# A fused attention, LayerNorm, MLP and expert kernel: k and q are loaded where their places come free, q's parts get a second home, chained products keep to four banks, and the ring of streamed weights has five places

## The chip, the cores and the metric

The kernel runs on one core of a Trainium2 chip. The metric is the device time of one execution in microseconds (us), taken as the median of several runs. A core has a matrix engine (TensorE, PE in the rows), a vector engine (VectorE, DVE), a scalar engine (ScalarE, ACT), GpSimd (POOL) and SyncE (SP), which here only issues transfers (DMAs). Each engine has an instruction queue of its own and waits for the others by semaphores.

## The reference

Three layers follow each other on 8 batches of 576 rows; all numbers are float32.

```python
def _attn_ref(q, k, v):                  # 8 batches, 8 heads, 576 x 64
    q_s = softmax(q, axis=-1)            # over the 64 of a head
    k_s = softmax(k, axis=2)             # over the 576 rows
    kv = np.einsum('bhsd,bhse->bhde', k_s, v)
    return np.einsum('bhsd,bhde->bhse', q_s, kv)

def _moe_ref(x, g_ln, w_ch1, w_ch2):     # x: 8 x 576 x 512
    mu = np.mean(x, axis=-1, keepdims=True)
    var = np.mean((x - mu) ** 2, axis=-1, keepdims=True)
    xn = (x - mu) / np.sqrt(var + 1e-06) * g_ln
    ch = np.maximum(xn @ w_ch1, 0.0) @ w_ch2      # 512 to 2048 to 512
    return x + ch
...
# third layer: 4 causal attention heads as experts, of which each row takes its best 2
```

## The kernel before, in words

Every float32 operand of a product is split into two rounded halves, so that a product is three matmuls (high by high, high by low, low by high). The matmul that fills most of the time has 128x128 weights and 128x288 moving columns, 288 being half (h = 0, 1) of a batch's rows.

**Units.** A head pair of a batch is a unit, n = 4 x batch + pair (class Heads). Its work comes in six steps: row maxima of k, softmax of k (k_exp writes ke), softmax of q (q_scale writes qe for head j = 0 and 1), turning q (pq, then qT = its high part by ACT and its low part by DVE), kv_product (pkv, at whose start the last 128 rows of q are turned too), then po, the pair's result. v has two homes, one for even and one for odd units. kv_product ends by issuing the loads of k, q and v of the unit two further on; these go through SyncE, whose queue keeps the written order (manual_schedule). The other engines' instructions are put in order by the framework's scheduler.

**LayerNorm** (class Norm) works on one half at a time: pmu (the mean by a matmul), the squares (ACT, added on GpSimd), pvar, root, scaling, and then class Mix, which makes the sums of blocks that the MLP needs (b11, t1, t2, b22, t3, b21, t4; tiles xm, xw_a, xw_b). front_slots says at which slots of the previous batch's matmul pieces the steps of units and LayerNorm are called: NORM_GAP = 8 slots lie between the two halves.

**MLP.** The hidden layer has 16 blocks of 128. From batch 2 (FAST) on, 12 of them are done by Strassen-Winograd with 7 products in place of 8, in three groups of four blocks (fast_group). A product j (0 to 6) for i = 0, 1 is six matmuls. Products chain in three accumulators: pa (j = 0, 2, 4, 6), pc (j = 1, 3), pb (j = 5). DVE adds parts that ACT copied before (total, tmp), ACT takes relu and the rounded high part, DVE or GpSimd the low part: these are the hidden parts hid0 and hid1. Behind each group, `second` sums eight accumulators of 12 matmuls each from four hidden parts, and DVE adds each one to xT. bank() hands PSUM banks to pa, pb, pc and acc in rotation over six.

**Streamed weights.** The weights of a group's seven products are sums of weight blocks, made once (class Sums, its pieces pinned into the slots of batch 1) and kept in device memory as w_d. They are read again for each batch, 21 per batch, through a ring of six places (class Stream); fill(), called behind each product, issues loads as long as their places are free. I write W0, W1, ... for them: W28 to W34 are the seven of batch 3's group 1.

In time: batch 0 and 1 take the first 237 us, batches 2 to 7 follow until about 775 us, and the third layer takes the rest, which the diff doesn't touch.

## Time and profile before

| what | value |
|---|---|
| median of 3 runs | 1348.7 us (1347.04 to 1350.21) |
| profiled execution, its own time | 1347.08 us |
| its span, first to last instruction | 1345.4 us |
| mean granted TensorE clock | 0.992 |
| PE busy | 1289.7 us (96%) |
| DVE, ACT, POOL busy | 956.9 (71%), 762.0 (57%), 460.6 us (34%) |

The span is what the trace covers; the execution's own time is 1.7 us longer. PE is busy for 96% of it, so a change of the order can win only what PE waits, and what it loses when its clock is lowered.

### The profile page before, as it was taken

Reading aid. Unit: us, or ns where it says so; the run is one execution under the profiler, and the core shown is the slowest. Engines: PE = TensorE matmul, PEld = TensorE weight load, DVE = VectorE, ACT = ScalarE, POOL = GpSimd, SP = SyncE. Lnnn points to the kernel's source line nnn. Section 1 sums busy time; section 2 is a strip of 40 time slices with the busy share of each in tenths; the row PEclk is TensorE's granted clock in tenths of the full one; section 3 lists DMA queues with packets and bytes.
Section 4 is the critical chain, followed back from the end, with each engine's and each line's share of the span. In section 5 each row is a group of like instructions: output and inputs, shape, how many; then the busy total and the mean of one; then the engine's idle time right before and its main releaser. Section 6 shows DMA issues by size and latency. Waiting matters only on the chain.

```text
span 1345.4 us, 27550 instructions
## 1 busy us (share of the span) xinstructions
PE 1289.7 (96%) x9907; PEld 1239.7 (92%) x9907; DVE 956.9 (71%) x2704; ACT 762.0 (57%) x1956; POOL 460.6 (34%) x568
## 2 busy tenths in 40 slices
PE   6999999699989999999998999999999999999998
PEld 5889999699979999999998999999999999999996
DVE  6885776866858769678487447777777777777774
ACT  6875444544555556455466235656565666666665
POOL 6675345433444335434346101112121112121222
PEclk9999999899989999999999999999999999999999
DMA  9763375965755657657458224333323242333122
GB/s 244 222 213 96 120 250 168 321 184 176 236 174 193 211 184 256 193 200 237 126 194 279 64 62 139 87 110 86 106 73 104 81 110 94 90 107 91 44 50 73
DMA packets 173416, 203.53 MB, mean 151 GB/s; under 512 B 93152, under 2 KB 137696, under 8 KB 170976
## 3 DMA queue, kind: packets, MB, share of 16 engines
q1 hardware_dynamic: 150656, 164.80, 41.0%
q10 hardware_dynamic: 22624, 36.97, 7.5%
q8 instruction: 79, 1.29, 0.4%
q14 instruction: 57, 0.47, 0.1%
HBM read 140.13 MB, written 46.40 MB: 139 GB/s over the span
## 4 chain that ended last, share of the span: by engine, by line
PE 67%; DVE 11%; DMA 7%; ACT 3%; issue 2%; POOL 2%; SPq 1%; ACTq 0%; DVEq 0%; POOLq 0%
PE acc L191 14%; PE psh L191 11%; PE psqk L191 7%; PE psc L191 7%; PE pssc L191 4%; PE pa L194 4%; PE py L191 4%; PE pso L191 4%; PE psv L191 4%; PE pst L1827 3%; DMA q<-in_q_dram 2%; PE pc L194 2%; DVE xc L692 1%; DMA k<-in_k_dram 1%; DMA wraw<-in_moe_w_ch_dram 1%
## 5 line engine op out<-in xcount | busy, mean ns | idle before, releaser
L191 PE MATMUL psh<-xhl,w 128*128 128x288 f32 x1248 | 188.6, 298 | 1.3 <-DVE xhl L701 1.0
L191 PEld LDWEIGHTS psh<-xhl,w 128*128 128x128 f32 x1248 | 172.2, 188 | 3.9 <-DVE xhl L701 1.5
L1810 POOL TENSOR_SCALAR sm<-sm,st,lg 128x128 f32<-128x128 f32 (+3 forms) x128 | 82.5, 655 | 263.7 <-DVE lg L1727 62.3
L191 PE MATMUL acc<-xw_b,w 128*128 128x288 f32 x912 | 137.4, 298 | 5.6 <-POOL xw_b L1325 3.4
L191 PE MATMUL acc<-xw_a,w 128*128 128x288 f32 x912 | 138.5, 297 | 3.4 <-DVE tmp L1328 1.7
L191 PEld LDWEIGHTS acc<-xw_b,w 128*128 128x128 f32 x912 | 125.7, 188 | 8.2 <-POOL xw_b L1325 4.8
L191 PEld LDWEIGHTS acc<-xw_a,w 128*128 128x128 f32 x912 | 126.3, 188 | 5.0 <-DVE xw_a L313 2.9
L191 PE MATMUL psqk<-x,wqk 128*128 128x288 f32 x768 | 112.9, 297 | 0.4 <-DVE k L1630 0.4
L191 PEld LDWEIGHTS psqk<-x,wqk 128*128 128x128 f32 x768 | 105.1, 188 | 1.6 <-PE pst L1827 0.6
L1391 DVE TENSOR_TENSOR xT<-xT,acc 128x288 f32<-128x288 f32 x152 | 66.2, 448 | 50.0 <-PE acc L191 49.6
L191 PE MATMUL psc<-hb,w 128*128 128x288 f32 x672 | 100.2, 298 | 0.0
L1798 ACT ACTIVATE sm<-sm,st 128x128 f32<-128x128 f32 (+3 forms) x144 | 83.9, 584 | 20.5 <-DVE st L1790 19.0
L191 PEld LDWEIGHTS psc<-hb,w 128*128 128x128 f32 x672 | 92.1, 188 | 0.3
L191 PE MATMUL acc<-hh,w 128*128 128x288 f32 x576 | 89.3, 300 | 2.9 <-DVE hh L798 1.5
L191 PEld LDWEIGHTS acc<-hh,w 128*128 128x128 f32 x576 | 79.8, 188 | 6.2 <-DVE hh L798 3.0
L1325 POOL TENSOR_TENSOR xw_b<-tmp,xw_b 128x288 fp32r<-128x288 f32 x72 | 61.3, 864 | 69.2 <-ACT xw_b L1324 49.9
L1851 ACT ACTIVATE aTh<-pst 128x128 fp32r<-128x128 f32 (+4 forms) x224 | 70.2, 333 | 23.4 <-PE pst L1827 10.9
L1852 DVE TENSOR_TENSOR aTl<-pst,aTh 128x384 fp32r<-128x384 f32 (+3 forms) x196 | 72.4, 381 | 11.4 <-ACT aTh L1851 9.0
L1790 DVE CUSTOM_DVE_ANT_0 sm<-pssc,mask 128x128 f32<-128x128 f32 (+2 forms) x144 | 67.9, 482 | 15.7 <-PE pssc L191 6.5
L645 POOL TENSOR_TENSOR sq<-sq 128x288 f32<-128x288 f32 x42 | 37.5, 894 | 91.0 <-ACT sq L676 89.0
L507 POOL TENSOR_TENSOR qe<-q,sm 128x320 f32<-128x320 f32 x64 | 46.8, 751 | 43.9 <-PE pkv L546 30.5
L191 PE MATMUL pssc<-k,q 128*128 128x128 f32 (+3 forms) x256 | 59.2, 327 | 0.0
(268 smaller groups left out, 3160.7 us busy)
## 6 DMA issues: line engine op xcount, KB each, us to landing
w_r<-w_d SPq DMA_DIRECT2D x76, 512.0 KB, 5.2
xw_b<-w_d SPq DMA_DIRECT2D x42, 512.0 KB, 4.8
wraw<-in_moe_w_ch_dram SPq DMA_DIRECT2D x32, 512.0 KB, 4.6
xhl<-xn_d SPq DMA_DIRECT2D x14, 1152.0 KB, 5.0
xp_d<-xT ACTq DMA_DIRECT2D x16, 576.0 KB, 5.0
k<-k SPq DMA_DIRECT2D x32, 288.0 KB, 3.5
k<-in_k_dram SPq DMA_DIRECT2D x32, 256.0 KB, 3.6
q<-in_q_dram SPq DMA_DIRECT2D x32, 256.0 KB, 4.0
```

The lines of the kernel that those rows point to most:

```text
L191: nc.tensor.matmul(o, lhsT, rhs, start=start, stop=stop)
L194: nc.tensor.matmul(o, lhsT, rhs, start=start, stop=stop, skip_group_check=True)
L507: nc.gpsimd.tensor_tensor(self.qe[:, :, j, :], self.qt[:, j], self.sm[:, 2, j * NCH:(j + 1) * NCH, None].to_broadcast([P, NCH, D]), op=ALU ...
L645: nc.gpsimd.tensor_tensor(self.t, self.t, self.sq[:, c], op=ALU.add)
L1325: nc.gpsimd.tensor_tensor(u[:, 1], src, raw(u[:, 0]), op=ALU.subtract)
L1391: nc.vector.tensor_tensor(xs[:, c], xs[:, c], ps, op=ALU.add)
L1790: nc.vector.tensor_tensor_reduce(out=sm[:m, c0:c1], in0=o_, in1=msk, scale=1.0, scalar=3e38 if n == 0 else st[:m, j, 0:1], op0=ALU.add, op ...
L1798: nc.scalar.activation(sm[:m, :w], sm[:m, :w], AF.Exp, bias=st[:m, j, last:last + 1], scale=-1.0, accum_out=st[:m, j, 2:3])
L1810: nc.gpsimd.tensor_scalar(sm[:m, :w], sm[:m, :w], st[:m, j, 3:4], self.gate()[:, j:j + 1], op0=ALU.mult, op1=ALU.mult)
L1827: nc.tensor.transpose(pt[:kw, kb * m:kb * m + m], sm[:m, kb * P:kb * P + kw], ident[:m, :m])
L1851: nc.scalar.activation(oh, from_, AF.Copy)
L1852: nc.vector.tensor_tensor(ol, from_, raw(oh), op=ALU.subtract)
```

## The change

k of the unit two further on is loaded right behind k_exp, and its q right behind the second q_scale; only v stays in kv_product. qT of odd units lies in a place of its own. pvar has its own bank from batch 3 on. bank() gives fixed banks: pa 0 and 1, pc and pb together 2 and 3, and `second` follows a table in which -1 is one bank of ps_m; it sums the hidden parts in the order 0, 2, 1, 3. The ring has five places; the memory of the sixth goes to qT. Batch 2's LayerNorm halves lie 6 slots apart instead of 8, and Sums(p) is called from slot 1 + 4p instead of 1 + 5p.

```diff
@@ class Heads
         def k_exp(self):
...
             nc.scalar.activation(self.ke.rearrange("p c j d -> p j c d"), self.kt, AF.Exp)
+            if next_unit(self.n) >= 2 * NPR:
+                load(next_unit(self.n), "k")
...
             nc.gpsimd.tensor_tensor(self.qe[:, :, j, :], self.qt[:, j],
...
+            if j == 1 and next_unit(self.n) >= 2 * NPR:
+                load(next_unit(self.n), "q")
...
-                    self.qT = self.tile([P, 2, S], "qT", F32 if self.whole else F32R, bufs=self.wide)
+                    if qt_odd and self.n % 2:
+                        self.qT = qt_odd[0].tile([P, 2, S], F32R, tag="qT", name=f"qT{self.n}")
+                    else:
+                        self.qT = self.tile([P, 2, S], "qT", F32 if self.whole else F32R, bufs=self.wide)
...
             if next_unit(self.n) >= 2 * NPR:
-                load_qk(next_unit(self.n))
                 load_v(next_unit(self.n))
@@ class Norm
-            ps = psy(nm)[:, :T]
+            ps = (lnbank[0] if lnbank and nm == "pvar" else psy(nm))[:, :T]
@@ front_slots
-                slots.setdefault(t + NORM_GAP * h + i, []).append(g)
+                slots.setdefault(t + (6 if b == FAST else NORM_GAP) * h + i, []).append(g)
@@ last_space
-        for i in range(2):
-            ring[MIDB + i] = cut(t, 12 * T + 8 * P * i, WSL)
+        ring[MIDB] = mixp.tile(WSL, F32R, tag="w", name="w_r")
+        qt_odd.append(mixp)
...
+        lnbank.append(ps_m.tile([P, 512], F32, tag="m", name="pvar"))
@@ bank
-    def bank(name):
-        taken[0] += 1
-        n = taken[0] % 6
-        if n < 2:
-            return ps_m.tile([P, 512], F32, tag="m", name=name)[:, :T]
-        return ps_acc.tile([P, 512], F32, tag=f"acc{n - 2}", name=name)[:, :T]
+    def bank(name, n):
+        if n < 0:
+            if not main:
+                main.append(ps_m.tile([P, 512], F32, tag="m", name="acc"))
+            return main[0][:, :T]
+        return ps_acc.tile([P, 512], F32, tag=f"acc{n}", name=name)[:, :T]
+
+    main = []
+    SBANK = (-1, 2, 3, 0, 1, -1, 2, 3)
@@ fast_group
-                d[nm] = bank("p" + nm)
+                d[nm] = bank("p" + nm, i if nm == "a" else 2 + i)
@@ plain_group
-            ps = bank("psh")
+            ps = bank("psh", (0, 1, 2, 3, -1)[(4 * (1 - h) + f) % 5])
@@ second
-            ps = bank("acc")
+            ps = bank("acc", SBANK[4 * (1 - h) + c])
-            for i in range(4):
+            for n, i in enumerate((0, 2, 1, 3)):
@@ the ring and the slots of Sums
-        ring.extend([None, None])
+        ring.append(None)
...
-            slots.setdefault(1 + 5 * p + i, []).append(pinned(piece))
+            slots.setdefault(1 + 4 * p + i, []).append(pinned(piece))
```

How the order moves is shown at three places. The first is SyncE's queue in batch 3's group 1, ahead of the load of v of unit 21 (home v_140; v_136 is that of unit 20); before, W28 to W33 are already issued above these rows, and the last row begins with W34, the weight of j = 6.

```order
L401 DMA k_5680<-in_k_dram 128x2x64
L399 DMA q_5683<-in_q_dram 128x2x256
L401 DMA q_5683<-in_q_dram 128x2x64
L412 DMA v_136<-in_v_dram 112x4x64 x2
L414 DMA v_136<-in_v_dram 128x2x64
L399 DMA k_5799<-in_k_dram 128x2x256
L401 DMA k_5799<-in_k_dram 128x2x64
L399 DMA q_5802<-in_q_dram 128x2x256
L401 DMA q_5802<-in_q_dram 128x2x64
L412 DMA v_140<-in_v_dram 112x4x64 x2
L414 DMA v_140<-in_v_dram 128x2x64
L1294 DMA w_r<-w_d 128x1024 x3
```

In the changed kernel the same place reads as follows; the first row is W32, and the last begins with W33, the weight of j = 5.

```order
L1308 DMA w_r<-w_d 128x1024
L412 DMA v_136<-in_v_dram 112x4x64 x2
L414 DMA v_136<-in_v_dram 128x2x64
L399 DMA k_5714<-in_k_dram 128x2x256
L401 DMA k_5714<-in_k_dram 128x2x64
L399 DMA q_5723<-in_q_dram 128x2x256
L401 DMA q_5723<-in_q_dram 128x2x64
L412 DMA v_140<-in_v_dram 112x4x64 x2
L414 DMA v_140<-in_v_dram 128x2x64
L1308 DMA w_r<-w_d 128x1024 x14
```

k and q stay in front of v, but they now come from the middle of units 18 and 19, and one weight fewer (W33) stands ahead of the v load of unit 21.

The second is PE behind unit 19's pkv (batch 3, group 1) before; po is unit 19's result, pa is product j = 6 on W34.

```order
L191 MATMUL pkv_4697<-v_140,ke_4629 64x66 x10
L191 MATMUL po_4749<-qT_4680,kv_1958 128x288 x3
L191 MATMUL po_4754<-qT_4680,kv_1958 128x288 x3
L194 MATMUL pa<-xm,xw_b 128x288 x12
L191 MATMUL pmu<-lnsum,mean_r 128x288
L194 MATMUL pa<-xm,xw_b 128x288 x12
L191 MATMUL pmu<-lnsum,mean_r 128x288
```

After the change, from the same pkv (here pkv_4703; acc is the one accumulator of `second` in the bank of ps_m) to pb, which is product j = 5 on W33, and to pa, j = 6:

```order
L191 MATMUL pkv_4703<-v_140,ke_4630 64x66 x10
L191 MATMUL acc<-hid,w_4_157 128x288 x3
L191 MATMUL acc<-hid,w_6_593 128x288 x2
L191 MATMUL po_4749<-qT_4686,kv_1961 128x288 x2
L191 MATMUL acc<-hid,w_6_593 128x288
L191 MATMUL acc<-hid,w_5_158 128x288 x3
L191 MATMUL acc<-hid,w_7_594 128x288
L191 MATMUL po_4749<-qT_4686,kv_1961 128x288
L191 MATMUL po_4754<-qT_4686,kv_1961 128x288 x3
L191 MATMUL acc<-hid,w_7_594 128x288 x2
L194 MATMUL pb<-xm,w_r 128x288 x12
L194 MATMUL pa<-xm,w_r 128x288 x12
```

Before, the six matmuls of po stood between pkv and the first product on a weight that is issued behind v; now 18 do, the six of po and twelve of an accumulator.

The third is PE around the mean (pmu) of the second LayerNorm half of batch 2, among the last matmuls of batch 1 (acc sums of hidden blocks w_9, w_10, w_11; psh the last hidden block itself). Before:

```order
L191 MATMUL acc_2732<-hh,w_10_594 128x288
L191 MATMUL acc_2733<-hh,w_10_594 128x288
L191 MATMUL acc_2734<-hh,w_10_594 128x288
L191 MATMUL acc_2731<-hh,w_10_594 128x288 x2
L191 MATMUL pmu<-lnsum,mean_r 128x288
L191 MATMUL acc_2732<-hh,w_10_594 128x288 x2
L191 MATMUL acc_2733<-hh,w_10_594 128x288 x2
L191 MATMUL pmu<-lnsum,mean_r 128x288
L191 MATMUL acc_2734<-hh,w_10_594 128x288 x2
L194 MATMUL pa<-xm,w_r 128x288
```

After the change:

```order
L191 MATMUL psh<-xhl,w_6_592 128x288 x8
L191 MATMUL pmu<-lnsum,mean_r 128x288
L191 MATMUL psh<-xhl,w_6_592 128x288 x3
L191 MATMUL pmu<-lnsum,mean_r 128x288
L191 MATMUL psh<-xhl,w_6_592 128x288
L191 MATMUL acc_2757<-hh,w_9_596 128x288
L191 MATMUL acc_2758<-hh,w_9_596 128x288
L191 MATMUL acc_2759<-hh,w_9_596 128x288
L191 MATMUL acc_2760<-hh,w_9_596 128x288
L191 MATMUL acc_2757<-hh,w_9_596 128x288 x2
```

Both pmu now stand ahead of the sums of block w_9, before they stood within those of w_10: 34 matmuls earlier.

## Rows read from the trace of the kernel before

**Rows 1.** Table by stage; columns: stretch, length, busy per engine (count), clock, DMA, GB/s.

```profile
0.00:225.00 225.00, 209.24 (x1690) 195.08 (x1691) 162.74 (x317) 135.96 (x288) 126.09 (x138) 0.99 0.63 187
225.00:775.00 550.00, 516.03 (x4062) 500.75 (x4060) 383.30 (x762) 287.77 (x667) 227.13 (x234) 0.98 0.62 201
775.00:1346.00 571.00, 564.44 (x4160) 543.83 (x4158) 410.86 (x1627) 338.26 (x1001) 107.39 (x197) 1.00 0.31 89
```

**Rows 2.** What PE waited for, 225 to 775: total, times, longest.

```profile
PE pa L194 <- DVE tmp L1328: 2.3, 3, 1.2
PE pkm L462 <- DVE qT L532: 2.3, 2, 1.3
...
PE pc L194 <- DVE xm L201: 1.4, 2, 1.2
```

**Rows 3.** PE's timeline, batch 1 to 2: start, length, instruction; in brackets idle before, releaser.

```profile
234.78 0.29 PE L191 MATMUL pmu<-lnsum,mean_r 128*128 128x288 f32 x1
...
237.53 0.40 PE L194 MATMUL pa<-xm,w_r 128*128 128x288 f32 x1 [1.54 <-ACT xm L200]
...
242.26 0.40 PE L191 MATMUL pvar<-lnsum,mean_r 128*128 128x288 f32 x1 [1.10 <-ACT lnsum L649]
...
245.12 0.57 PE L540 MATMUL pq<-ident,qe 112*128 112x112 f32 x4 [1.64 <-DVE k L489]
247.72 0.47 PE L546 MATMUL pkv<-ident,qe 128*128 128x128 f32 x1 [2.02 <-DVE qT L532]
...
250.81 0.47 PE L480 MATMUL pkm<-ident,cm 128*128 128x128 f32 x1 [0.91 <-DVE cm L471]
254.27 0.85 PE L194 MATMUL pc<-xm,w_r 128*128 128x288 f32 x2 [2.99 <-ACT xm L200]
```

**Rows 4.** PE's timeline behind pkv of the last unit, batches 2 to 5.

```profile
297.43 0.53 PE L191 MATMUL acc<-xw_b,w 128*128 128x288 f32 x2 [1.52 <-ACT xw_b L1324]
...
388.07 0.80 PE L191 MATMUL pkv<-v,ke 112*64 112x66 f32 x20
392.28 1.12 PE L191 MATMUL po<-qT,kv 128*128 128x288 f32 x6 [3.41 <-ACT kv L570]
395.12 3.25 PE L194 MATMUL pa<-xm,xw_b 128*128 128x288 f32 x12 [1.72 <-DMA xw_b<-w_d]
...
483.71 0.79 PE L191 MATMUL acc<-xw_b,w 128*128 128x288 f32 x4 [2.39 <-POOL xw_b L1325]
...
485.15 1.75 PE L194 MATMUL pa<-xm,w_r 128*128 128x288 f32 x12
...
566.07 1.06 PE L191 MATMUL acc<-xw_b,w 128*128 128x288 f32 x6 [0.51 <-POOL xw_b L1325]
568.83 0.66 PE L191 MATMUL acc<-xw_a,w 128*128 128x288 f32 x3 [1.70 <-DVE tmp L1328]
```

**Rows 5.** SyncE's queue (issues), batch 3 and, last row, batch 4.

```profile
385.85 0.47 SPq L401 DMA_DIRECT2D q<-in_q_dram  x1
388.79 1.59 SPq L412 DMA_DIRECT2D v<-in_v_dram  x2
...
391.08 0.93 SPq L1294 DMA_DIRECT2D xw_b<-w_d  x2
...
478.78 1.24 SPq L412 DMA_DIRECT2D v<-in_v_dram  x2
```

**Rows 6.** Table by stretch, as rows 1.

```profile
393.80:400.60 6.80, 5.47 (x23) 5.48 (x24) 2.01 (x5) 2.22 (x6) 1.38 (x2) 0.51 1.03 404
482.00:484.00 2.00, 0.29 (x2) 0.29 (x3) 1.62 (x5) 1.02 (x4) 1.65 (x3) 1.00 0.87 277
```

**Rows 7.** Timeline of ACT's queue and of GpSimd, batch 1 to 2.

```profile
233.27 3.49 ACTq L1228 DMA_DIRECT2D w_d<-w  x3
...
239.01 2.72 POOL L645 TENSOR_TENSOR sq<-sq 128x288 f32<-128x288 f32 x3 [8.42 <-ACT sq L676]
```

**Rows 8.** ACT's timeline behind pkv at batch 3.

```profile
391.92 0.31 ACT L570 ACTIVATE kv<-pkv,ks 64x64 fp32r<-64x64 f32 x1 [0.34 <-DVE kv L574]
```

More of the change, by code (lines that the diff above doesn't have):

```diff
@@ L336, in tile_kernel @@
     ap = p1r.enter_context(pool("a", 2, side="right"))
-    spare, idle = [], []
+    spare, idle, lnbank = [], [], []
     def psy(name):
@@ L358, in whole @@
         return n < WHOLE
-    vbuf, kvbuf, kvwhole = [], [], []
+    vbuf, kvbuf, kvwhole, qt_odd = [], [], [], []
     for i in range(NPR):
@@ L401, in load @@
         nc.sync.dma_start(out=t[:, :, NIL, :], in_=rows(S - P, [[D, P], [S * D, 2], [1, D]]))
-        loaded.setdefault(n, []).append(t)
+        loaded.setdefault(n, {})[nm] = t
     def load_v(n):
@@ L425, in __init__ @@
             self.pl = unit_pool(n)
-            self.kt, self.qt = loaded.pop(n)
+            t = loaded.pop(n)
+            self.kt, self.qt = t["k"], t["q"]
             self.vt = vbuf[unit_buf(n)]
@@ L1164, in tile_kernel, with half_tiles @@
     w1b = {}
-    def half_tiles(pl, f0):
-        w1b[f0] = pl.tile([P, HALF, 2, NDC, P], F32R, tag=f"w1_{f0}", name=f"w1_{f0}")
+    p1b = ExitStack()
+    def half_tiles(pl, f0, pl1=None):
+        w1b[f0] = (pl1 or pl).tile([P, HALF, 2, NDC, P], F32R, tag=f"w1_{f0}", name=f"w1_{f0}")
         return [x for i in range(HALF) for x in fc_tiles(pl, f0 + i, w1b[f0][:, i])]
@@ L1174, in more_weights @@
         p0.close()
-        later.append(p1.enter_context(pool("w_b")))
-        blocks.extend(half_tiles(later[0], HALF))
+        later.append(p1.enter_context(pool("w_b2")))
+        later.append(p1b.enter_context(pool("w_b1")))
+        blocks.extend(half_tiles(later[0], HALF, later[1]))
     wide = Wide(blocks, mid, hp, 0)
@@ L1264, in last_space @@
         x_pair(XORD[5:])
-        t = later[0].tile([P, HALF * 2 * NDC * P], F32R, tag=f"w1_{HALF}", name="xw_b")
-        xslot["b12"] = cut(t, 0, XSL)
-        hid1.extend(cut(t, (4 + 2 * i) * T, HSL) for i in range(4))
-        for i in range(2):
-            ring[MIDB + i] = cut(t, 12 * T + 8 * P * i, WSL)
+        p1b.close()
+        mixp = p1.enter_context(pool("mix"))
+        later.append(mixp)
+        xslot["b12"] = mixp.tile(XSL, F32R, tag="b12", name="xw_b")
+        t = mixp.tile([P, 4, 2, T], F32R, tag="hid", name="hid")
+        hid1.extend(t[:, i] for i in range(4))
+        ring[MIDB] = mixp.tile(WSL, F32R, tag="w", name="w_r")
+        qt_odd.append(mixp)
         stream.use(0, before_last + 7, ring)
@@ L1298, in tile_kernel @@
     stream = Stream()
-    taken = [0]
-    def bank(name):
-        taken[0] += 1
-        n = taken[0] % 6
-        if n < 2:
-            return ps_m.tile([P, 512], F32, tag="m", name=name)[:, :T]
-        return ps_acc.tile([P, 512], F32, tag=f"acc{n - 2}", name=name)[:, :T]
+    def bank(name, n):
[6 more added lines that the diff above has]
+    SBANK = (-1, 2, 3, 0, 1, -1, 2, 3)
     def fast_group(b, gr):
@@ L1382, in one @@
         def one(h, c):
[L1383 removed]
+            ps = bank("acc", SBANK[4 * (1 - h) + c])
             sl = slice(c * P, (c + 1) * P)
[L1385 removed]
+            for n, i in enumerate((0, 2, 1, 3)):
                 wt, u = w2s[f0 + i], (hid0, hid1)[h][i]
[L1387 removed]
+                mm(ps, wt[:, 0, sl], u[:, 0], n == 0, False)
                 mm(ps, wt[:, 0, sl], u[:, 1], False, False)
[L1389 removed]
+                mm(ps, wt[:, 1, sl], u[:, 0], False, n == 3)
             xs = xTs[b][:, :, h * T:(h + 1) * T]
@@ L1500, in tile_kernel @@
             t = t.rearrange("p a b c -> p (a b c)")
-            stream.use(before_last + 7, before_last + 7 * NG, [cut(t, 8 * P * i, WSL) for i in range(2)] + ring[MIDB:])
+            stream.use(before_last + 7, before_last + 7 * NG, [cut(t, 8 * P * i, WSL) for i in range(2)] + ring[MIDB:] +
+                       [later[2].tile(WSL, F32R, tag="qT", name="w_r")])
             wcp = late.enter_context(pool("w_c", side="right"))
```

2 lines of the change are left out of this document (removed).

## The prediction

> **What bounds the kernel now.** The table of stages comes first: TensorE (PE) works 209 of the first 225 us and 564.44 of the last 571, but 516.03 of the 550 between, so 34.0 us of idle lie where the change works, and the granted clock is lowest there too (0.98) [rows 1]. The view of what PE waited for in that middle part shows no main culprit: one to three waits for each of many releasers [rows 2]. So I went to PE's timeline and found two knots.
>
> The first is the passage from batch 1 to batch 2. Six waits of 1.54, 1.10, 1.64, 2.02, 0.91 and 2.99 us stand between 236 and 254.3, 10.2 us in all, while PE has hardly anything else to do [rows 3]. They are one chain: the LayerNorm's second half needs pmu (234.78), its squares are added on GpSimd at 239.0 to 241.7, then pvar (242.26), and the first chained product (pc) can start at 254.27, when ACT has made xm.
>
> The second comes once in each of the batches 2 to 5, behind the last head pair's product pkv: 1.52; 3.41 and 1.72; 2.39; 0.51 and 1.70, together 11.25 us [rows 4]. At batch 3 it reads best. pkv ends at 388.87. SyncE's queue runs in written order; it held the load of v until pkv had read the old v, issued it at 388.79, and only then (391.08) the streamed weights written behind it [rows 5]. pa starts on these weights at 395.12, 6.25 us behind pkv. At the other three v takes about 0.35 us less to issue (1.24 against 1.59), so 6.0 is the usual lag. Here the clock fell as well: from 393.8 to 400.6 it was at 0.51 of full, its lower level (1.2 of 2.4 GHz), and 5.47 us of work were done at it, so 2.7 us were lost [rows 6]. At 482 to 484, with a single wait of 2.39, it stayed at 1.00.
>
> What is left of the 34.0, 12.5 us, is scattered: pa behind DVE's total 2.3, pkm behind DVE's qT 2.3, pc behind DVE's xm 1.4 [rows 2], and smaller ones.
>
> **The change, part by part.**
>
> *LayerNorm steps of batch 2 at gap 6, Sums at 4p.* In the new order both pmu of the second half stand 34 matmuls earlier on PE. A matmul of this shape takes 0.14 us (twelve in 1.75, the tail of the last included) [rows 4], hence 4.5 to 5 us; I take 4.5. The chain behind pmu keeps its length (7.5 to pvar, 12.0 on to pc), so pc moves from 254.27 to about 249.8. Two things take some back. pb, whose first 11 matmuls stand around those of pc before, comes later in the new order and covers less; I count 0.2. And ACT is held by three DMA issues of Sums for 3.49 us from 233.27 [rows 7]; the new order has them ahead of the squares, but something of this may meet the earlier chain: 0.5. Result **-3.8 us**. Bounds: 0, if the chain of the head pair (pkm, pq, pkv, which has 4.57 of the waits) sets the time, and -7, if it also moves out of the way.
>
> *k and q loaded early.* Each unit's four DMAs remain; they leave the place just ahead of v and move past the streamed weights in front of it on SyncE's queue. At 0.47 us each [rows 5] they hold it 1.9 us. At batch 3 they were out of it by 386.32, 2.5 us ahead of v, which waited for pkv alone, so taking them away from there frees nothing behind pkv; in their new place they delay by 1.9 us at most a weight whose product is one to four products away: 0. But one streamed weight moves with them: with the ring of five, the weight that stands behind the last v load is that of the product j=5 (pb), not j=6 (pa). In the new PE order 18 matmuls stand between pkv and pb (12 of one accumulator, 6 of po), 2.5 us. The weight still lands 6.0 behind pkv, so PE idles 3.5, at four places 14.0 against 11.25: **+2.8**. Before, the rotation of banks let up to four accumulators of `second` fill in; now only the one with a bank of its own can, as pb shares the banks of pc. Bounds: po waits for kv anyway, which ACT finishes at 392.23, 3.4 behind pkv [rows 8]; po stands 0.7 behind pkv, so 2.7 a place, 10.8 in all, is the least (-0.4). The most is that GpSimd's half of a hidden part, on which that accumulator waits as at 483.71, is late by the same 2.39 and comes on top: +9.6 more.
>
> *The clock at these four places.* Idle of 3.5 in 6.0 us stands between what kept the clock (2.39) and what lost it (3.41 and 1.72). One place falls now; I count one and a half, half a fall more at 2.7: **+1.4**. Bounds: none (-2.7) and all four (+8.1).
>
> *Second home of qT, own bank for pvar, fixed banks, LayerNorm.* pkm waited twice for DVE's qT while the first home was taken (2.3); pa waited three times for a bank that DVE had still to read (2.3), and with banks 0 and 1 of its own it follows accumulators that were finished several products before; pc behind xm (1.4) goes as the LayerNorm of batches 3 on has more matmuls between pvar and pa. That is 6.0; I take a quarter off, because what starts earlier may meet its next operand: **-4.5**. Bounds 0 and -6.0.
>
> *pb on pc's bank, one bank for two accumulators.* pb must now wait until DVE has read pc. In the new order 2 to 3 us of products lie between, which cover it; if that cover is gone, a wait costs what pa's cost, 0.77 (2.3 in three). I count one in 18 groups: **+0.6** (rounded down). Bounds 0 and 13.9.
>
> *Order 0, 2, 1, 3 of the hidden parts* only changes which part an accumulator needs first: GpSimd's waits at 483.71 are what it touches, counted above. The last batch's ring and phase 2 keep their work: 0.
>
> Sum: -3.8 + 2.8 + 1.4 - 4.5 + 0.6 = **-3.5 us**. The profiled execution took 1347.08 us (span 1345.4), 1.6 below the median of the three runs, 1348.7; the waits are of that execution, and the difference is applied to the median: **1345.2 us**.
>
> **Rivals.** What a measurement of this kernel can tell from no change is about 0.2%, that is 1346.0 to 1351.4.
>
> *Slower: the clock falls at every queued weight.* Each of the four places now has two idles in a row (po behind kv, about 2.7, then pb behind its weight, 0.8), as only batch 3 had. For it: that row is the only one of this pattern, and there the clock fell. Against it: the total idle was 5.1 there, 3.5 now. Price +8.1 in place of +1.4: +3.2, **1351.9**. It decides from the fourth fall on (with three the sum is +0.5). The Trainium skill (TensorE: Matmul & The Clock Gate, HAM oscillation) says that a kernel which waits for a transfer in each round starts each round at the low clock again. The rows at 393.8 agree with it, those at 482 do not: a wait of 2.39 left the clock alone.
>
> *No difference: the passage at 237 doesn't shorten.* The head pair's chain takes the place of the LayerNorm's. For it: 1.64, 2.02 and 0.91 are its waits and the pair's load isn't moved ahead of pvar on PE. Against it: pkm stands behind pvar in both orders, so it is pvar that holds it. Without the -3.8 the sum is +0.3: **1349.0**.
>
> *Slower by more: fixed banks make the chained groups wait.* If each of the 18 groups waits once for 0.77 and nothing of the -4.5 comes: -3.8 + 2.8 + 1.4 + 13.9 = +14.3, **1363.0**; half as many, 1356. For it: the four banks now have fewer free at once, and DVE is 70% busy in this part (383.30 of 550) [rows 1]. Against it: several products lie between a bank's two uses in the new order. The Trainium skill (Perfetto Trace Analysis, Matmuls, under Optimizing Tensor Performance) wants independent groups of matmuls to rotate through different banks so that reading one overlaps the next; that speaks for this rival. The trace bears it out only in part: with the rotation pa still waited for DVE's total three times.
>
> *Much faster.* The least idle at the four places (-0.4), no fall (-2.7), all 6.0 of the scattered waits gone, no new one: -12.9, **1335.8**.
>
> **How the numbers follow.** The likeliest, 0.45, with a range of its own from 1341 to 1349; no difference at the passage 0.16; clock falls everywhere 0.17; banks wait 0.10; much faster 0.12. Of the likeliest's 0.45 about 0.29 lie below 1346.0, 0.14 within, 0.02 above; the passage rival adds 0.03 below, 0.11 within and 0.02 above, the clock rival 0.05 within and 0.12 above, banks 0.10 above, much faster 0.11 below and 0.01 above as its waits may be given back. Faster 0.43, same 0.30, slower 0.27. The range 1337 to 1354 leaves out the banks' rival and the lower part of the much faster one, and holds the clock's.
>
> **What the profile after would show.** Right: pc of batch 2 starts near 250 and the waits ahead of it sum to about 6.5; behind pkv of batches 2 to 5 a wait of po for kv and one of pb for its weight, 3.5 together; pkm waits for qT nowhere; one or two stretches at half clock after 290. Wrong: pb waits for DVE's total in many groups; more than two stretches at half clock; pq or pkv of the pair at 240 waiting as long as now; another load than v ahead of a weight that PE waits for.

## The result and the profile after

The changed kernel takes 1358.85 us in the median of 5 runs (1356.88 to 1363.46), the kernel before 1348.7 on the same chip: ratio 1.0083, 95% interval 1.0061 to 1.0104. (Ratios, here and below, are taken over all undisturbed runs of both kernels and lie up to 0.1% off the quotient of the medians, which is 1.0075 here.) It is slower by 0.8%; the forecast was 1345.2, range 1337 to 1354.

The profiled execution took 1363.46 us, 4.6 more than the median. Of the 16.4 us by which it lies above the profiled execution of before, 3.6 arise in the first 147 us, ahead of the work that the change touches; the profiles of its variants below lack them, all but one. I leave these 3.6 out.

The page's line of busy time, and the row of the table by stage for 225 to 775, which answers to [rows 1] and has its columns (busy time of PE, of its weight loads, DVE, ACT and GpSimd, then granted clock, busy share of the DMA engines, GB/s):

```profile
PE 1305.5 (96%) x9907; PEld 1254.6 (92%) x9907; DVE 960.0 (70%) x2704; ACT 763.2 (56%) x1956; POOL 460.6 (34%) x568
```

```profile
225.00:775.00 550.00, 517.70 (x4017) 503.60 (x4017) 382.83 (x755) 290.11 (x670) 228.50 (x236) 0.97 0.62 200
```

Between 225 and 775 PE is idle for 32.3 us, against 34.0 before. So the change removed about as many waits as it added, and yet time was lost there. The table of single stretches (columns as before; the granted clock is the third value from the end) shows what got worse:

```profile
254.00:270.00 16.00, 10.48 (x61) 9.15 (x62) 13.18 (x22) 8.61 (x18) 9.70 (x7) 0.57 0.80 246
306.00:314.00 8.00, 6.78 (x31) 6.79 (x32) 3.16 (x8) 2.90 (x8) 4.25 (x6) 0.57 0.88 326
...
486.00:496.00 10.00, 7.40 (x35) 6.86 (x36) 5.18 (x13) 4.85 (x14) 5.17 (x7) 0.66 0.81 286
```

Five stretches run for a good part at the lower level (1.2 of 2.4 GHz), three of which are shown; before there were two, at the passage and in batch 3 (393.8 to 400.6 [rows 6]). Summed over rows of 2 us of the same table (a row at 0.75 counts half its busy time as done at the lower level), PE did 29.1 us of its work at that level, against 10.9 before. Such work takes nearly twice as long (twelve matmuls of pa took 3.25 us at the lower level and 1.75 at the full one [rows 4]), so about half of the difference, 9.1 us, is what the clock cost: 7.4 of it at the four places behind pkv, 1.7 at the passage.

The rest was lost earlier, in batch 1, where PE had none of these waits before. PE's timeline, with the idle time before an instruction and its releaser in brackets:

```profile
189.53 0.32 PE L481 MATMUL pkm<-ident,cm 128*128 128x128 f32 x1 [0.61 <-DVE cm L472]
190.84 0.79 PE L191 MATMUL acc<-hh,w 128*128 128x288 f32 x4 [0.98 <-ACT hh L802]
...
192.72 1.32 PE L191 MATMUL acc<-hh,w 128*128 128x288 f32 x8 [0.50 <-DVE hh L805]
...
205.55 0.32 PE L481 MATMUL pkm<-ident,cm 128*128 128x128 f32 x1 [1.49 <-DVE cm L472]
...
207.75 0.82 PE L191 MATMUL po<-qT,kv 128*128 128x288 f32 x2 [1.30 <-ACT hh L802]
```

These five are 4.9 us. The clock fell behind them as well, which by the rows from 206 to 212 adds about 1.5; one of these rows:

```profile
208.00:210.00 2.00, 2.00 (x9) 2.00 (x10) 1.89 (x4) 1.85 (x4) 0.00 (x0) 0.50 0.79 260
```

At equal work PE comes out of batch 1 7.3 us later than before. DVE's timeline shows what pkm waited for:

```profile
185.51 0.82 DVE L453 TENSOR_REDUCE sm<-q 128x10 f32<-128x640 f32 x1 [2.72 <-DMA q<-in_q_dram]
186.25 0.97 DVE L540 TENSOR_TENSOR qT<-pq,qT 128x448 fp32r<-128x448 f32 x1
187.12 1.70 DVE L1214 TENSOR_TENSOR w_x<-w 128x512 f32<-128x512 f32 x2
...
189.21 0.27 DVE L472 TENSOR_REDUCE cm<-pkm 128x1 f32<-128x128 f32 x1
```

DVE waits 2.72 us for a q that lands late, then turns to the unit's qT, and then to the first step of Sums (L1214, w_x, 1.70 us), which stands ahead of the rest; the column maximum (cm) that PE waits for comes out at 189.5. In the same unit before, DVE's timeline has the short wait for q, and the step of Sums (there L1204) only behind the column maximum:

```profile
179.61 0.82 DVE L452 TENSOR_REDUCE sm<-q 128x10 f32<-128x640 f32 x1 [0.67 <-DMA q<-in_q_dram]
...
183.84 0.27 DVE L471 TENSOR_REDUCE cm<-pkm 128x1 f32<-128x128 f32 x1
...
187.03 1.29 DVE L1204 TENSOR_TENSOR w_x<-w 128x512 f32<-128x512 f32 x2
```

At the passage from batch 1 to 2 six others stand in place of the six waits of [rows 3], 9.1 us instead of 10.2:

```profile
253.89 0.33 PE L554 MATMUL pkv<-ident,qe 128*128 128x128 f32 x1 [2.26 <-DVE qT L540]
...
256.08 0.48 PE L463 MATMUL pkm<-ident,km 128*128 128x128 f32 x1 [1.12 <-DMA q<-in_q_dram]
257.83 0.85 PE L194 MATMUL pc<-xm,w_r 128*128 128x288 f32 x2 [1.28 <-ACT xm L200]
...
262.86 2.77 PE L194 MATMUL pc<-xm,w_r 128*128 128x288 f32 x10 [2.14 <-DVE xm L201]
```

pc is held now by DVE (2.14 for xm) and pkv by DVE's qT (2.26). And behind the last pkv of batches 2 to 5 (the first is shown, in the timelines of PE, GpSimd and SyncE's queue):

```profile
307.22 1.09 PE L191 MATMUL acc<-hid,w 128*128 128x288 f32 x3 [3.54 <-POOL hid L1340]
...
310.76 2.57 PE L194 MATMUL pb<-xm,w_r 128*128 128x288 f32 x10
```

```profile
303.80 1.26 POOL L456 TENSOR_TENSOR q<-q,sm 128x640 f32<-128x640 f32 x1 [1.61 <-DVE sm L453]
305.01 1.40 POOL L510 TENSOR_TENSOR qe<-q,sm 128x320 f32<-128x320 f32 x2
306.37 2.31 POOL L1340 TENSOR_TENSOR hid<-tmp,hid 128x288 fp32r<-128x288 f32 x3
```

```profile
304.80 2.63 SPq L1308 DMA_DIRECT2D w_r<-w_d  x5
```

The accumulator that should fill in waits 3.54 us for a hidden part from GpSimd, and GpSimd had the q steps of the next unit (L456, L510) to do first. At the other places part of the wait is for a hidden part from ACT (1.22 and 2.01). The weight behind v was issued at 304.80; pb, which needs it, starts at 310.76 without a wait of its own. The waits at the four places are 3.54; 1.22, 1.54 and 0.32; 2.01 and 1.53; 0.97, 1.46 and 0.38, together 12.97, against 11.25 before [rows 4].

At the start of each of the batches 3 to 6 stands a new wait of 1.0 to 1.4 us, 4.9 in all, that the trace gives no releaser for:

```profile
356.68 1.03 PE L194 MATMUL pc<-xm,w_r 128*128 128x288 f32 x6 [1.25 <-issue]
```

```profile
354.80 0.75 DVE L201 TENSOR_TENSOR xw_a<-xc,xw_a 128x576 fp32r<-128x576 f32 x1
355.47 0.75 DVE L201 TENSOR_TENSOR xm<-xc,xm 128x576 fp32r<-128x576 f32 x1
356.13 0.81 DVE L1406 TENSOR_TENSOR xT<-xT,acc 128x288 f32<-128x288 f32 x2
```

This pc takes the bank of `second`'s last accumulators. DVE adds those to xT in the row of 356.13 (two of them in 0.81 us), behind two LayerNorm splits (L201). Half of 0.81 puts the first of the two at 356.53, and pc starts at 356.68: it is DVE that holds it, by that working.

### The profile page after: what moved, and what is told of

Same layout as the page of the kernel before. It is cut to its first block, busy times and chain, and to the rows that moved or that the text cites. A ratio compares the mean times of both kernels' runs of the same rounds, so it can differ in the third digit from the quotient of the medians.

```text
span 1361.7 us, 27542 instructions
## 1 busy us (share of the span) xinstructions
PE 1305.5 (96%) x9907; PEld 1254.6 (92%) x9907; DVE 960.0 (70%) x2704; ACT 763.2 (56%) x1956; POOL 460.6 (34%) x568
## 3 DMA queue, kind: packets, MB, share of 16 engines
q8 instruction: 79, 1.29, 0.4%
## 4 chain that ended last, share of the span: by engine, by line
PE 79%; DVE 6%; DMA 3%; ACT 2%; issue 1%; SPq 1%; POOL 0%; DVEq 0%; ACTq 0%; POOLq 0%
PE acc L191 20%; PE psh L191 11%; PE psqk L191 7%; PE psc L191 7%; PE pa L194 7%; PE pssc L191 4%; PE py L191 4%; PE pso L191 4%; PE psv L191 4%; PE pc L194 3%; PE pst L1843 3%; PE pb L194 2%; DMA q<-in_q_dram 2%; PE po L191 2%; PE pkv L191 1%
## 5 line engine op out<-in xcount | busy, mean ns | idle before, releaser
L191 PE MATMUL acc<-hid,w 128*128 128x288 f32 x912 | 139.5, 303 | 13.6 <-POOL hid L1340 9.0
L191 PEld LDWEIGHTS acc<-hid,w 128*128 128x128 f32 x912 | 128.5, 192 | 16.0 <-POOL hid L1340 10.1
L191 PE MATMUL acc<-xw_a,w 128*128 128x288 f32 x918 | 129.9, 296 | 0.0
L1340 POOL TENSOR_TENSOR hid<-tmp,hid 128x288 fp32r<-128x288 f32 x72 | 62.9, 881 | 85.0 <-ACT hid L1339 61.4
L194 PE MATMUL pa<-xw_a,w_r 128*128 128x288 f32 x408 | 65.0, 301 | 1.6 <-ACT xw_a L200 1.0
L194 PE MATMUL pa<-xm,w_r 128*128 128x288 f32 x408 | 63.8, 298 | 1.1 <-DVE pw L272 1.1
```

Source lines behind the costliest of these rows:

```text
L191: nc.tensor.matmul(o, lhsT, rhs, start=start, stop=stop)
L194: nc.tensor.matmul(o, lhsT, rhs, start=start, stop=stop, skip_group_check=True)
L1340: nc.gpsimd.tensor_tensor(u[:, 1], src, raw(u[:, 0]), op=ALU.subtract)
```

## The experiments

Five parts were suspected: Sums at 1 + 4p, the early loads of k and q, the ring of five, the fixed banks, the gap of 6. Each was undone in the changed kernel or put into the kernel before alone, and then in pairs. All ratios are to the kernel before, run on the same chip in the same session.

**Sums back to 1 + 5p**

```diff
-            slots.setdefault(1 + 4 * p + i, []).append(pinned(piece))
+            slots.setdefault(1 + 5 * p + i, []).append(pinned(piece))
```

> The changed kernel with the Sums called from slot 1 + 5p again. Theory A (the earlier Sums put their GpSimd, DVE and ACT work and their transfers on top of the units of batch 1, so that q lands later and PE waits): the waits between 170 and 215 us (0.61, 0.98, 0.50, 1.49, 1.30, with a stretch at half clock) go, and about 6 us of the loss: near 1353. Rival B (the early loads of k and q make these waits): the waits stay, the time stays within 1 us of 1358.9.

Measured: 1354.04 us, ratio 1.0016 (0.9997 to 1.0035). The waits in batch 1 are gone, though the early loads are still there: it is Sums that makes them.

**Gap of 8 again**

```diff
-                slots.setdefault(t + (6 if b == FAST else NORM_GAP) * h + i, []).append(g)
+                slots.setdefault(t + NORM_GAP * h + i, []).append(g)
```

> The changed kernel with 8 slots between the LayerNorm halves of batch 2, as before. If the gap of 6 shortened the passage from batch 1 to batch 2 as predicted (-3.8 us), the time rises to about 1362 and pvar waits longer again. If another chain took its place, as the trace of the changed kernel suggests (passage shorter by 0.4 only), the time stays within 1.5 us.

Measured: 1361.13, ratio 1.0066 (1.0046 to 1.0085). Not told apart from the changed kernel: the gap is not worth 3.8 us here.

**Rotation over six banks again**

```diff
-    def bank(name, n):
-        if n < 0:
...
+        taken[0] += 1
+        n = taken[0] % 6
...
-        lnbank.append(ps_m.tile([P, 512], F32, tag="m", name="pvar"))
```

> The changed kernel with the rotation over six banks again and without pvar's own bank. Theory C (fixed banks: pc waits until DVE has read the last accumulators, 4.9 us in four places, and only one accumulator can fill in behind pkv, 13.0 us with the clock at half in four places): the four waits of pc go, the places behind pkv fall back to about 11 us and one half clock, the time falls by 8 to 12 us, to about 1349. Rival D (the early loads bring the next unit's q steps ahead on GpSimd, and these delay the hidden parts): only the waits of pc go, about 1354, and PE still waits for GpSimd's hidden parts behind pkv.

Measured: 1356.24, ratio 1.0040 (1.0019 to 1.0061). The waits of pc at the batch starts go. The places behind pkv still wait (3.2 us in batch 2, 3.2 in batch 3) and all four still run at the lower clock, so the fixed banks are not what makes PE wait there. But they decide what it waits for: with the rotation, in batches 3 and 4, it is po for kv (2.35 in both) and then pb for its weight (0.85 and 1.42), the pair of waits that the prediction had worked out. In place of pc's waits pb waits for its weights 0.6 to 1.0 us at three batch starts.

**k and q loaded late again**

```diff
-            if next_unit(self.n) >= 2 * NPR:
-                load(next_unit(self.n), "k")
...
-            if j == 1 and next_unit(self.n) >= 2 * NPR:
-                load(next_unit(self.n), "q")
...
             if next_unit(self.n) >= 2 * NPR:
+                load_qk(next_unit(self.n))
                 load_v(next_unit(self.n))
```

> The changed kernel with k and q loaded in kv_product again, ahead of v. Theories A and C: batch 1 keeps its waits, the places behind pkv too; within 2 us of 1358.9. Rival B: the waits between 170 and 215 go, about -6. Rival D: the waits for GpSimd's hidden parts behind pkv shrink, about -5 to -8.

Measured: 1357.37, ratio 1.0035 (1.0018 to 1.0053). Batch 1 keeps its waits, and PE still waits for GpSimd's hidden parts behind pkv (3.06 and 1.45 in batch 2), so the early loads make neither. The ratio is 0.5% below the changed kernel's 1.0083: the waits of pc at the starts of the batches are gone, and batch 3 keeps the full clock.

**One part alone in the kernel before: the ring of five**

```diff
-        ring.extend([None, None])
+        ring.append(None)
...
-        for i in range(2):
-            ring[MIDB + i] = cut(t, 12 * T + 8 * P * i, WSL)
+        ring[MIDB] = cut(t, 12 * T, WSL)
+        sixth.append(cut(t, 12 * T + 8 * P, WSL))
```

> The kernel before with a ring of five places, and nothing else changed (the memory of the sixth place is left for the last batch). Theory E (the ring of five puts pb's weight behind the load of v, so that behind pkv of batches 2 to 5 PE has 18 matmuls instead of 24 to 54 before the first product on a late weight, waits 3 to 4 us at each place and loses the clock there): the order behind pkv is the changed kernel's, the time rises by 5 to 8 us, ratio 1.004 to 1.006. Rival C (the fixed banks alone do it): within 1.5 us of the kernel before.

Measured: 1353.26, ratio 1.0023 (1.0005 to 1.0041). The order behind pkv is nearly the changed kernel's (15 to 18 matmuls of accumulators and po, then pb). The waits, too, are for hidden parts, here in PE's timeline in batch 2; in batches 3 to 5 po waits 0.97 for kv and pb 0.27 to 0.81 for its weight besides:

```profile
295.16 0.87 PE L191 MATMUL acc<-xw_b,w 128*128 128x288 f32 x3 [1.65 <-POOL xw_b L1326]
298.02 1.81 PE L191 MATMUL acc<-xw_b,w 128*128 128x288 f32 x6 [2.00 <-POOL xw_b L1326]
```

Four places run at the lower clock instead of one. The size is less than expected, because the worst place of before, that of batch 3, gets better by 4.5 us at equal work while the others lose 4.8, 4.1 and 2.6.

**Alone: Sums from 1 + 4p**

```diff
-            slots.setdefault(1 + 5 * p + i, []).append(pinned(piece))
+            slots.setdefault(1 + 4 * p + i, []).append(pinned(piece))
```

> The kernel before with Sums from slot 1 + 4p, and nothing else. Theory A: the waits of batch 1 (pkm for cm, acc for hh, 170 to 215 us) appear, +5 to +9 us, ratio 1.004 to 1.0065. Rival (they need the other parts of the change beside them): within 1.5 us.

Measured: 1358.25, ratio 1.0068 (1.0051 to 1.0085). PE's timeline has the waits of the changed kernel, in the same places, though nothing else was changed:

```profile
185.95 0.32 PE L480 MATMUL pkm<-ident,cm 128*128 128x128 f32 x1 [0.60 <-DVE cm L471]
...
201.83 0.32 PE L480 MATMUL pkm<-ident,cm 128*128 128x128 f32 x1 [1.35 <-DVE cm L471]
```

**Alone: early loads**

```diff
+                load(next_unit(self.n), "k")
...
+                load(next_unit(self.n), "q")
...
-                load_qk(next_unit(self.n))
                 load_v(next_unit(self.n))
```

> The kernel before with the early loads of k and q, and nothing else. Theory F (the early loads let the front of the next units go ahead on DVE at the passage from one batch to the next, where DVE is full, and delay what reads the accumulators): +3 to +6 us, with waits of pc or pa for DVE at the start of the batches 3 to 6. If the loads are hidden both ways, as the prediction had it: within 1.5 us.

Measured: 1351.17, ratio 1.0008 (0.9993 to 1.0023). With the rotation of banks the early loads cost 0.2% at most, and perhaps nothing.

**Undone: Sums and the ring of five together**

The sixth place takes back the memory of qT's second home, which is left out here and in all versions of the changed kernel with a ring of six.

```diff
-            slots.setdefault(1 + 4 * p + i, []).append(pinned(piece))
+            slots.setdefault(1 + 5 * p + i, []).append(pinned(piece))
...
-        ring[MIDB] = mixp.tile(WSL, F32R, tag="w", name="w_r")
-        qt_odd.append(mixp)
+        for i in range(2):
+            ring[MIDB + i] = mixp.tile(WSL, F32R, tag=f"w{i}", name="w_r")
...
-        ring.append(None)
+        ring.extend([None, None])
```

> The changed kernel with Sums from 1 + 5p and a ring of six places, whose sixth takes the memory of qT's second home, which is left out. Theories A and E: nothing is left of the waits in batch 1 and little of those behind pkv; 6 to 8 us below the run with 1 + 5p alone, ratio to the kernel before 0.996 to 0.998. If the fixed banks made the waits behind pkv (theory C), they stay, ratio about 1.0016 as with 1 + 5p alone.

Measured: 1357.5, ratio 1.0062 (1.0039 to 1.0086). A miss. The waits behind pkv are gone (the largest left is 1.29), but pc now waits 2.3 to 2.7 us for xm at the starts of the four batches 4 to 7, each with the clock down. Something that is left takes back more than the ring gave.

**Alone: gap of 6**

```diff
-                slots.setdefault(t + NORM_GAP * h + i, []).append(g)
+                slots.setdefault(t + (6 if b == FAST else NORM_GAP) * h + i, []).append(g)
```

> The kernel before with 6 slots between the LayerNorm halves of batch 2, and nothing else: the prediction's step on the passage by itself. If LayerNorm's chain sets the passage: pc near 250 instead of 254.3, -3 to -4 us, ratio 0.997. Theory G (DVE sets it: it is busy all of 248 to 252, and an earlier LayerNorm only puts its scaling ahead of the unit's qT on DVE): pc no earlier than 253, ratio 0.999 to 1.001.

Measured: 1346.90, ratio 0.9982 (0.9969 to 0.9994). The passage itself is not shorter in PE's timeline:

```profile
240.23 0.53 PE L191 MATMUL pvar<-lnsum,mean_r 128*128 128x288 f32 x1 [1.07 <-ACT lnsum L649]
...
244.84 0.58 PE L540 MATMUL pq<-ident,qe 112*128 112x112 f32 x4 [1.01 <-DVE k L489]
248.72 3.25 PE L194 MATMUL pb<-xm,xw_b 128*128 128x288 f32 x12 [3.31 <-DMA xw_b<-w_d]
...
253.54 0.72 PE L194 MATMUL pc<-xm,w_r 128*128 128x288 f32 x2
```

pvar comes 2 us earlier than in [rows 3], but pq still waits for DVE until 244.84 (245.12 before), and pkv starts at 251.77 instead of 247.72, behind a pb that waits for its weight. The LayerNorm itself did come earlier: ACT has its part of xm ready at 249.46, where pc had to wait for it until 254.27 before. But pc stands behind pkv on PE and starts at 253.54. At equal work PE is 0.7 us ahead of before at 225 us and 1.2 behind at 282, so the passage got 1.9 us longer. What was gained lies in batch 3.

**Sums back, and rotation; Sums back, and late loads; Sums back, rotation and ring of six.** The edits are those above, put together:

```diff
-            slots.setdefault(1 + 4 * p + i, []).append(pinned(piece))
+            slots.setdefault(1 + 5 * p + i, []).append(pinned(piece))
...
+        n = taken[0] % 6
```

> The changed kernel with Sums from 1 + 5p and the rotation over six banks (no own bank for pvar). Theory C for the waits of pc only: they cost what they show, 3 to 5 us, and go; the places behind pkv stay as they are with a ring of five: ratio 0.997 to 0.999, against 1.0016 with 1 + 5p alone. If the fixed banks gain elsewhere what they cost here: 1.001 to 1.003.

Measured: 1355.13, ratio 1.0061 (1.0036 to 1.0086). A miss: with a ring of five and 1 + 5p the rotation is no gain.

```diff
-            slots.setdefault(1 + 4 * p + i, []).append(pinned(piece))
+            slots.setdefault(1 + 5 * p + i, []).append(pinned(piece))
...
+                load_qk(next_unit(self.n))
                 load_v(next_unit(self.n))
```

> The changed kernel with Sums from 1 + 5p and k and q loaded in kv_product again. Theory F (early loads load DVE at the passages): the waits of pc at the starts of batches 3, 5 and 6 go, ratio 0.996 to 0.999. If the early loads are hidden both ways: 1.001 to 1.003, as with 1 + 5p alone.

Measured: 1348.54, ratio 0.9999 (0.9983 to 1.0016). The waits of pc at the batch starts are gone, but the gain over 1.0016 is 0.2%, and the intervals overlap.

```diff
-            slots.setdefault(1 + 4 * p + i, []).append(pinned(piece))
+            slots.setdefault(1 + 5 * p + i, []).append(pinned(piece))
...
+        n = taken[0] % 6
...
+        ring.extend([None, None])
```

> The changed kernel with Sums from 1 + 5p, the rotation over six banks and the ring of six (without qT's second home). What is left of the change is the early loads, the gap of 6 and the order 0, 2, 1, 3. If fixed banks together with the ring of six made LayerNorm late at the starts of the batches (the waits of pc for xm of 2.3 to 2.7 us with the ring of six alone), these go and the ratio is 0.995 to 0.999. If the early loads make them (theory F), they stay, 1.002 to 1.005.

Measured: 1339.07, ratio 0.9943 (0.9923 to 0.9963). Faster than both kernels. With the rotation, six places in exchange for qT's second home gain 1.2% (1.0061 to 0.9943); with the fixed banks they cost 0.5% (1.0016 to 1.0062). So ring and banks work on each other, and the last runs ask how.

**Alone: the fixed banks and pvar's own bank**

```diff
-                d[nm] = bank("p" + nm)
+                d[nm] = bank("p" + nm, i if nm == "a" else 2 + i)
...
-            ps = bank("acc")
+            ps = bank("acc", SBANK[4 * (1 - h) + c])
...
+        lnbank.append(ps_m.tile([P, 512], F32, tag="m", name="pvar"))
```

> The kernel before with the fixed banks and pvar's own bank, and nothing else; the ring keeps six places. If fixed banks cost something by themselves (theory C): waits of pc and pb at the starts of the batches, LayerNorm late there as with the ring of six in the changed kernel, ratio 1.004 to 1.008. If they only cost something with the early loads: 0.999 to 1.001.

Measured: 1336.22, ratio 0.9897 (0.9882 to 0.9912): the fastest kernel of the study, below both expectations. The place behind pkv in batch 3, where PE stood idle for 5.13 us before [rows 4], reads in its timeline

```profile
379.23 1.32 PE L194 MATMUL pb<-xm,w_r 128*128 128x288 f32 x8
...
381.68 0.40 PE L191 MATMUL acc<-xw_b,w 128*128 128x288 f32 x1 [0.74 <-ACT xw_b L1326]
382.50 4.61 PE L191 MATMUL acc<-xw_b,w 128*128 128x288 f32 x32 [0.42 <-DVE tmp L1330]
386.96 0.96 PE L191 MATMUL po<-qT,kv 128*128 128x288 f32 x6
```

Eight matmuls of pb and 36 of accumulators now stand between pkv and po; the waits are 0.74 and less. By the table of stretches only the passage is left at the lower clock, and PE is idle for 23.7 us from 225 to 775 instead of 34.0:

```profile
242.00:258.00 16.00, 10.28 (x56) 8.37 (x56) 13.60 (x23) 8.50 (x18) 8.43 (x6) 0.57 1.03 367
225.00:775.00 550.00, 526.33 (x4136) 510.52 (x4135) 384.19 (x768) 289.19 (x673) 229.82 (x234) 0.99 0.62 201
```

**The fastest of the undone versions, less one part each:** late loads, Sums from 1 + 4p, and the order 0, 1, 2, 3.

```diff
+                load_qk(next_unit(self.n))
                 load_v(next_unit(self.n))
```

> The fastest version so far (the changed kernel with 1 + 5p, the rotation over six banks and the ring of six; ratio 0.9943) with k and q loaded in kv_product again. If the early loads bring its gain: back to 0.998 to 1.000. If they bring nothing and the order 0, 2, 1, 3 and the gap of 6 do: 0.993 to 0.996.

Measured: 1340.47, ratio 0.9930 (0.9911 to 0.9949). The early loads bring nothing there.

```diff
-            slots.setdefault(1 + 5 * p + i, []).append(pinned(piece))
+            slots.setdefault(1 + 4 * p + i, []).append(pinned(piece))
```

> The fastest version so far with the Sums from 1 + 4p. Theory A: batch 1 loses its 7 us here too, whatever the rest is: ratio 1.000 to 1.002.

Measured: 1350.99, ratio 1.0010 (0.9996 to 1.0024). The loss by the earlier Sums is 0.7% here too.

```diff
-            for n, i in enumerate((0, 2, 1, 3)):
+            for n, i in enumerate((0, 1, 2, 3)):
```

> The fastest version so far with the hidden parts in the order 0, 1, 2, 3. If the order 0, 2, 1, 3 lets the accumulators behind pkv start on parts that are ready and so keeps the clock up there (its gain lies between 376 and 400 us): the stretch at half clock at 394 is back, ratio 0.997 to 1.000. If the order is of no account: 0.993 to 0.996.

Measured: 1351.10, ratio 1.0005 (0.9990 to 1.0020). The order brings the 0.6%: without it po waits 2.96 and pa 1.82 in batch 3 again, and the lower clock from 390 to 402 is back. This version is the kernel before with the early loads, the gap of 6 and the changed kernel's tiles, and is as fast as the kernel before.

**The fixed banks with a ring of five**

```diff
+            ps = bank("acc", SBANK[4 * (1 - h) + c])
...
-        ring.extend([None, None])
+        ring.append(None)
```

> The kernel before with the fixed banks and pvar's own bank (ratio 0.9897 by themselves) and a ring of five. If the ring of five takes the cover behind pkv (theory E), the gain goes: waits for hidden parts or po's kv and half clock at four places, ratio 0.998 to 1.003, so the ring costs about 1% beside fixed banks. If the fixed banks keep their gain: 0.990 to 0.993.

Measured: 1360.17, ratio 1.0082 (1.0057 to 1.0107). The ring of five takes the whole gain of the fixed banks and as much again, 1.9%. One wait of PE's timeline behind pkv in the batches 2, 3 and 5 (in batch 4 there is one of 2.00 for GpSimd):

```profile
296.18 1.81 PE L191 MATMUL acc<-xw_b,w 128*128 128x288 f32 x6 [1.99 <-POOL xw_b L1328]
...
386.27 0.66 PE L191 MATMUL acc<-xw_b,w 128*128 128x288 f32 x3 [2.70 <-POOL xw_b L1328]
...
565.63 0.45 PE L191 MATMUL acc<-xw_b,w 128*128 128x288 f32 x1 [1.94 <-ACT xw_b L1327]
```

In batch 3, 4 matmuls of pa and 4 of one accumulator stand between pkv and po there, in place of pb's 8 and the accumulators' 36: pb's weight is now the one behind v (pb starts at 388.70), and by the table of banks (SBANK) only an accumulator in the bank of ps_m, one at a time, needs none of the banks of pa, pb and pc.

**The fixed banks with the early loads**

```diff
+            ps = bank("acc", SBANK[4 * (1 - h) + c])
...
+                load(next_unit(self.n), "k")
...
+                load(next_unit(self.n), "q")
```

> The kernel before with the fixed banks, pvar's own bank and the early loads of k and q. If the early loads are what makes LayerNorm late at the starts of the batches beside fixed banks (2.3 to 2.7 us for xm in the run with the ring of six and 1 + 5p), the gain goes here too: 1.000 to 1.006. If they are hidden: 0.988 to 0.992.

Measured: 1352.05, ratio 1.0016 (0.9992 to 1.0041). The early loads take the gain away too, 1.2%, and they do it at the batch starts. PE's timeline at batch 3's and batch 4's, and DVE's at batch 3's:

```profile
344.30 2.77 PE L194 MATMUL pc<-xm,xw_b 128*128 128x288 f32 x10 [2.29 <-DVE xm L201]
...
427.78 6.57 PE L191 MATMUL acc<-xw_a,w 128*128 128x288 f32 x36 [2.45 <-DVE xT L1397]
```

```profile
332.20 1.31 DVE L449 TENSOR_REDUCE km<-k 128x128 f32<-128x640 f32 x1 [0.77 <-DMA k<-in_k_dram]
...
333.79 0.81 DVE L453 TENSOR_REDUCE sm<-q 128x10 f32<-128x640 f32 x1
...
337.68 0.81 DVE L499 TENSOR_REDUCE sm<-q 128x10 f32<-128x640 f32 x1
338.40 1.87 DVE L201 TENSOR_TENSOR xw_b<-xc,xw_b 128x576 fp32r<-128x576 f32 x1
...
340.56 1.81 DVE L201 TENSOR_TENSOR xw_a<-xc,xw_a 128x576 fp32r<-128x576 f32 x1
342.30 1.95 DVE L201 TENSOR_TENSOR xm<-sq,xm 128x576 fp32r<-128x576 f32 x1
```

While PE waits for xm, DVE splits LayerNorm's blocks (L201) behind three steps on k and q of a later unit (L449, L453, L499), 2.9 us in all. With the fixed banks alone DVE does none of these between 326 and 344; the split of xm is done there at 340.34 instead of 344.25, and pc doesn't wait for it.

## Why the prediction was wrong

I compared the profiles also at equal work: how much later than the kernel before each one is when PE has put through as many moving columns (us; the first column is the time at which before was there).

| before at | changed | Sums 4p alone | ring of five alone | fixed banks alone | banks, ring of five | banks, early loads |
|---|---|---|---|---|---|---|
| 174.7 | +3.6 | +0.3 | +0.2 | -0.5 | -0.4 | -1.7 |
| 215.0 (batch 1) | +10.9 | +7.4 | +0.3 | -0.5 | -0.2 | -1.6 |
| 281.7 (passage) | +10.0 | +5.3 | +0.2 | -1.0 | -0.4 | -1.5 |
| 299.7 (batch 2, behind pkv) | +14.5 | +8.7 | +5.0 | -1.6 | +2.3 | -2.0 |
| 376.9 | +13.1 | +9.2 | +2.6 | -2.3 | +2.3 | +1.6 |
| 408.0 (batch 3, behind pkv) | +8.2 | +9.3 | -2.2 | -10.7 | -4.2 | -6.3 |
| 497.6 (batch 4, behind pkv) | +12.0 | +9.0 | +3.1 | -10.9 | -1.8 | -1.9 |
| 576.1 (batch 5, behind pkv) | +16.5 | +8.3 | +6.6 | -11.2 | +3.8 | +1.7 |
| 834.8 | +16.7 | +9.0 | +7.0 | -10.4 | +8.6 | +4.5 |

Step by step:

- **Sums at 4p.** This is the step that failed first, and it cost the most. The prediction took the edit together with the gap and asked only whether ACT, held by the issues of Sums' transfers, would be late for LayerNorm's squares (0.5). It put nothing down for batch 1, where PE had no waits. By itself the edit costs 0.68%, undoing it gives 0.67%: some 9 us, 7.1 of them in batch 1 (from +0.3 to +7.4 in the table) and 3.4 behind pkv of batch 2, where the clock falls, with 2.1 given back at the passage. The cover that was not named is DVE's time between a unit's qT and its cm; Sums' first step, 1.7 us, now falls into it. The q that DVE waits for also lands about 2 us later (a wait of 2.47 with Sums alone, 0.67 before); what delays it was not tested.
- **The passage, -3.8.** Wrong; the rival "the passage doesn't shorten" was right. LayerNorm's chain came earlier, as worked out, but other waits took its place: those of the head pair's pq and pkv for DVE (1.34 and 2.26), as the rival had it, then a q that lands late (1.12) and DVE's part of xm (2.14); and the clock stays low for more work (8.7 us against 5.4). The changed kernel gains 0.9 us there by equal work (+10.9 to +10.0), and the gap of 6 alone loses 1.9.
- **The load of v and the ring of five, +2.8, and the clock, +1.4.** The sign and the place were right, and of the mechanism this: the weight that stands behind v is pb's, and little cover is left behind pkv. Wrong was what ends last there. Not the weight but a hidden part from GpSimd or ACT holds PE, and pb's weight has landed by then: pb waits at none of the four. I had put that wait down as the bound "+9.6 more" and not into the sum. The waits grew by 1.7 us only, but all four places lost the clock, which cost 7.4 us where the sum had 1.4. The rival "the clock falls at every queued weight" had that outcome and was given 0.17; its picture, po waiting for kv and then pb for its weight, came only with the rotation.
- **The early loads, 0.** Right beside the rotation of banks (1.0008), wrong beside the fixed banks, where they cost 1.2%, and in the changed kernel, where loading late again gives 0.5%. I looked at the queue they sit in and not at what an earlier k and q starts: the next unit's steps on DVE, at the starts of the batches, where LayerNorm needs it.
- **Fixed banks, second home, LayerNorm, -4.5, and pb on pc's bank, +0.6.** What the terms named came true in the changed kernel: the waits of pkm for qT and of pa for DVE's total, 2.3 each, are gone, and pb never waits for pc's bank. But pc's new waits at the batch starts, 4.9, take that back; no term of the sum had them, only the rival "fixed banks make the chained groups wait". And the main effect of the banks was missed. Alone the fixed banks and pvar's bank gain 1.03%, 14 us by the medians; of the 10.4 between the two profiles 8.4 arise behind pkv in batch 3 (from -2.3 to -10.7 in the table), where pb and the accumulators get in front of po. For the banks alone that rival had the opposite. The rule of the Trainium skill that stood beside it (Perfetto Trace Analysis, Matmuls, under Optimizing Tensor Performance) wants groups to rotate through banks; the runs agree only at four batch starts, with 4.9 us for pc.
- **Order 0, 2, 1, 3, 0.** Worth 0.6% in the version with the rotation and the ring of six; it was not run in the kernel before by itself.
- **Slips in the working.** One wait of 0.77 is +0.8 and not +0.6, and the shares of the chances add up to 0.31 for same and 0.26 for slower. Neither changes the outcome.

The five parts that were run alone sum to -0.22% (Sums +0.68, ring +0.23, loads +0.08, gap -0.18, banks -1.03), and the whole is +0.83%. The rest is between the parts, or in what was not run alone: the banks' gain needs pb and the accumulators behind pkv, which the ring of five takes away, and free time of DVE at the batch starts, which the early loads take. What stays open: why six places cost 0.5% beside fixed banks when the early loads are there too; why the rotation, which gains 0.4% in the changed kernel (the intervals touch), costs 0.45% once Sums is back at 1 + 5p; the share of qT's second home, which was not run by itself; and the places in memory that the diff gives to the hidden parts and one block of xm (the pool mix), which every version of the changed kernel keeps.
